# GpSimd without tensor work from routing on, and mish through one sigmoid, in a fused attention, expert and feed-forward kernel

## The chip, the cores and the metric

The kernel runs on one core of a Trainium2 chip. The metric is device time in microseconds (us), the median of several executions. The five engines of the core have queues of their own, each worked through strictly in the order in which the program wrote it, and they meet through semaphores: TensorE (PE in the profile; its weight loads are PEld), VectorE (DVE), ScalarE (ACT), GpSimd (POOL) and SyncE (SP), which here only starts DMA transfers.

## The reference

Three stages follow each other, each on the output of the one before. What is computed, shortened:

```
# 1. attention, 8 heads, 768 tokens, head_dim 64; only pairs in the same hash bucket count
scores = where(q_bucket == k_bucket, (q @ k.T) / 8, -1e9)
attn   = exp(scores - max);  attn /= sum + 1e-9
x      = attn @ v                                  # -> 768 x 512
# 2. mixture of 8 experts, top 1, at most 192 tokens an expert
logits = x @ w_gate;  expert = argmax(logits);  gate = softmax(logits)[expert]
y      = gate * (relu(x_e @ w1[e]) @ w2[e])        # w1: 8 x 512 x 1024, w2: 8 x 1024 x 512
# 3. a feed-forward network with mish
h      = y @ w_in                                  # 512 x 2048
sp     = where(h > 20, h, log1p(exp(min(h, 20))))
out    = (h * tanh(sp)) @ w_out                    # 2048 x 512
```

`w1` and `w2` come as float32, `w_in` and `w_out` as float64.

## The kernel before, in words

**Products in three terms.** Every float32 matrix that TensorE multiplies is split in two: a high part rounded to the type that TensorE takes (fp32r), and a low part, the rest. A product is three products: high by high, high by low, low by high. So each weight is loaded, its high part is cast (`wh`) and its low part subtracted (`wl`).

**Weights.** A chunk holds 1024 numbers per partition. Its raw numbers land in one of seven buffers (`raw`), which comes free when `wl` has been made. The high and low parts go into rings of six chunks. A float32 chunk of the experts (the key `w1` or `w2`) takes one cast (L573 on ScalarE or L575 on VectorE) and one subtraction (L580, on VectorE or GpSimd). A chunk of the second network (`wi`, `wo`) is float64 and comes in two halves; VectorE first rebuilds the float32 bits with three integer operations for each half (L552 and L554 in `w_bits`, L559 in `w_sign`), then follow cast and subtraction on 128x512. There are 64 chunks of the experts and 16 (32 halves) of the network. The first 13 chunks are loaded during attention, and the first six split there too.

**Routing.** From the logits VectorE works out each token's expert and its row there (L893 to L989, one-hot selection matrices `dg` at L947 among them); GpSimd then scatters the rows of x to memory (L953), from which SyncE loads them expert by expert (L1033).

**Experts.** In a step of the loop TensorE runs layer 1 of expert e+1 (L1064, 24 products with 512 columns) and layer 2 of expert e (L1106, 24 products with 512 columns), with transposes between (L1047): of the loaded rows, of the hidden units, and of the result. ScalarE and VectorE split each transposed block (`xh`/`xl`, `mhh`/`mhl`, `x2h`/`x2l`). Branches (L1198, L1152, L1166) skip rows beyond the first 128 of an expert where there are none. ScalarE also does relu (L1087) and the gate (L1123).

**Second network.** Sixteen steps f of 128 hidden units. Layer 1 of a step has two halves of 384 tokens, each of 12 products into one of two PSUM banks (`pg`, L1232); each half is then copied to the tile `hs_g` (L1242 on ScalarE or L1244 on VectorE), which frees the bank. mish then works on 128x768 numbers, and its result is split into `gh` (L1273) and `gl` (L1276). Layer 2 of a step has six token tiles of three products (`po`, L1282), which add up over all steps. Six tiles of `hs_g` exist, given back at `gl`: layer 1 of step f+6 cannot be copied out before `gl` of step f. There are four buffers `e_g`, four `n_g`, and the seven of `gh`/`gl`.

mish before, from h/2, with e = exp(min(h, 20)) and n = e(e + 2): mish = h n/(n + 2), where 1/(n/2 + 1) is exp(-ln(n/2 + 1)). For each step: `em` (VectorE), `e1` exp (ScalarE), `nn` (VectorE), `ln` (ScalarE), `e2` exp (ScalarE), `nm` (GpSimd, L1265, a product), `hm` (VectorE, L1268). A change between exp and ln makes ScalarE load another table first (ACT_TABLE_LOAD).

**What sets the order.** A planner (`Planner.run`) writes the queues. Each task has a duration for each engine that may do it, tasks that it waits for, and buffers that it takes and gives. Of all tasks that could begin, the one that could begin first by these durations is written next; a table of tuned numbers (`WHEN`, `FIRST`, `THEN`) only decides between those that could begin within 0.03 us of each other. `convert` makes the tasks of the weights, `expert_tasks` routing and experts, `network_tasks` the second network. In the second network the tasks of mish are tied in pairs of steps by `pair`.

## Time and profile before

| what | value |
|---|---|
| median of 3 runs (lowest to highest) | 484.14 us (482.75 to 484.5) |
| span of the profiled execution, first to last instruction | 481.0 us |
| median less that span | 3.1 us |
| PE, PEld busy | 426.2 us, 377.6 us |
| DVE, ACT, POOL busy | 407.6 us, 281.7 us, 196.7 us |
| mean granted TensorE clock | 0.951 |
| DMA over the span | 65.13 MB, mean 135 GB/s |

The profiled execution's own time is its span; no other time is listed for it, and the 3.1 us up to the median lie outside of what the trace shows. By TensorE's own instructions the span falls into attention (to about 154 us), routing (to 167), the experts (to 311), the second network (311 to 476) and the output (to 481). In a row of the timeline stand start, duration, engine, line, operation, what is written and read, and in square brackets how long the engine had been idle and what ended that. A row of a window gives its length, then for each engine the busy time and the number of instructions, then the granted TensorE clock, the DMA share and GB/s. In a row of groups stand busy time and mean duration in ns, then idle time before.

### The profile page before, as it was taken

The page shows a single profiled execution, that of the slowest core. Times are in us where ns is not written, and L with a number is a line of the kernel's source. Part 1 is how long each engine was busy: PE and PEld are TensorE (multiplying, and loading weights), DVE is VectorE, ACT ScalarE, POOL GpSimd, SP SyncE. Part 2 cuts the span into 40 slices and gives each one's busy share as a digit, 9 for nine tenths or more (in the row PEclk, how much of TensorE's full clock was granted, in tenths as well). Part 3 has the DMA queues.
Part 4 walks back from the last instruction along what each step waited for, and adds up shares of the span by engine and source line. Part 5 has one row for each costly group of instructions (what it writes and reads, how often), then busy time and mean ns, then how long its engine had stood idle before and what let it go on. Part 6 is the DMA issues. An engine that isn't in the chain of part 4 may idle for free. (4 is left out here: it accounts for less than half of the span.)

```text
span 481.0 us, 7356 instructions
## 1 busy us (share of the span) xinstructions
PE 426.2 (89%) x2628; PEld 377.6 (78%) x2628; DVE 407.6 (85%) x560; ACT 281.7 (59%) x483; POOL 196.7 (41%) x173
## 2 busy tenths in 40 slices
PE   7999999999999789899889895789697698599995
PEld 6999999999998767667667674788595697598784
DVE  6699999889886874949499999999999989999940
ACT  3598897787776234434445642428573674674552
POOL 5866575321001580406154524451518117107335
PEclk9799999999999899899999998889989599799998
DMA  6352532423000367958378878454213204200003
GB/s 183 116 181 85 163 117 83 133 68 106 5 1 1 133 172 232 347 191 275 124 269 277 303 272 310 142 191 167 104 49 131 90 0 174 89 0 1 0 0 131
DMA packets 30136, 65.13 MB, mean 135 GB/s; under 512 B 4752, under 2 KB 7824, under 8 KB 30096
## 3 DMA queue, kind: packets, MB, share of 16 engines
q1 hardware_dynamic: 28944, 61.44, 38.9%
q0 software_dynamic: 1152, 3.16, 1.7%
q8 instruction: 24, 0.39, 0.3%
q14 instruction: 16, 0.13, 0.1%
HBM read 58.26 MB, written 6.33 MB: 134 GB/s over the span
## 5 line engine op out<-in xcount | busy, mean ns | idle before, releaser
L580 POOL TENSOR_TENSOR wl<-raw,wh 128x1024 fp32r<-128x1024 f32 (+1 forms) x43 | 92.6, 2161 | 162.7 <-ACT wh L573 137.8
L573 ACT CAST wh<-raw 128x1024 fp32r<-128x1024 f32 (+1 forms) x70 | 59.8, 874 | 38.1 <-DVE raw L559 30.6
L580 DVE TENSOR_TENSOR wl<-raw,wh 128x1024 fp32r<-128x1024 f32 (+1 forms) x53 | 78.3, 1503 | 1.4 <-ACT wh L573 1.2
L1232 PE MATMUL pg<-x2h,wh 128*128 128x384 f32 x128 | 46.8, 365 | 11.9 <-ACT hs_g L1242 7.1
L700 DVE TENSOR_REDUCE nm<-ps 128x1 f32<-128x768 f32 x48 | 45.5, 950 | 6.8 <-PE ps L694 6.5
L732 DVE TENSOR_TENSOR atl<-pt,ath 128x512 fp32r<-128x512 f32 x72 | 46.7, 683 | 3.6 <-ACT ath L727 3.5
L1232 PE MATMUL pg<-x2l,wh 128*128 128x384 f32 x128 | 45.8, 358 | 2.5 <-DVE x2l L1145 2.5
L708 ACT ACTIVATE a<-ps,nm 128x768 f32<-128x768 f32 x48 | 44.1, 918 | 4.4 <-DVE nm L700 4.4
L1232 PE MATMUL pg<-x2h,wl 128*128 128x384 f32 x128 | 45.2, 353 | 0.0
L727 ACT CAST ath<-pt 128x512 fp32r<-128x512 f32 x72 | 39.0, 595 | 6.9 <-PE pt L722 6.5
L1282 PE MATMUL po<-wh,gh 128*128 128x512 f32 x96 | 38.1, 397 | 5.1 <-ACT gh L1273 5.1
L1265 POOL TENSOR_TENSOR n_g<-n_g,e_g 128x768 f32<-128x768 f32 x16 | 33.6, 2119 | 19.1 <-ACT e_g L1262 19.0
L1282 PE MATMUL po<-wh,gl 128*128 128x512 f32 x96 | 37.9, 395 | 2.4 <-DVE gl L1276 2.4
L722 PE MATMUL pt<-identf,a 128*128 128x128 f32 x288 | 38.5, 275 | 0.2 <-ACT a L708 0.2
L1282 PE MATMUL po<-wl,gh 128*128 128x512 f32 x96 | 37.9, 395 | 0.0
L744 PE MATMUL pa<-ath,vn 128*128 128x256 f32 x144 | 37.4, 295 | 0.5 <-ACT ot L632 0.5
L1232 PEld LDWEIGHTS pg<-x2h,wh 128*128 128x128 f32 x128 | 26.0, 203 | 14.1 <-ACT hs_g L1242 8.4
L554 DVE SCALAR_TENSOR_TENSOR raw<-raw,full 128x512 int32<-128x512 int32 x32 | 35.1, 1098 | 2.0
L744 PE MATMUL pa<-atl,vn 128*128 128x256 f32 x144 | 35.5, 282 | 0.0
L575 DVE CAST wh<-raw 128x1024 fp32r<-128x1024 f32 x26 | 27.2, 1060 | 7.4 <-PE ph L1064 4.7
L722 PEld LDWEIGHTS pt<-identf,a 128*128 128x128 f32 x288 | 32.1, 141 | 1.4 <-ACT a L708 0.5
L1106 PE MATMUL py<-wh,mhh 128*128 128x512 f32 (+1 forms) x72 | 28.1, 391 | 0.9 <-ACTq L1166 0.6
(199 smaller groups left out, 1086.1 us busy)
## 6 DMA issues: line engine op xcount, KB each, us to landing
raw<-in_moe_w_dram SPq DMA_DIRECT2D x64, 512.0 KB, 4.7
raw<-in_moe_w_in_dram SPq DMA_DIRECT2D x16, 512.0 KB, 4.2
raw<-in_moe_w_out_dram SPq DMA_DIRECT2D x16, 512.0 KB, 3.9
slots<-zt SPq DMA_DIRECT2D x12, 258.0 KB, 4.6
xs<-slots SPq DMA_DIRECT2D x8, 258.0 KB, 7.2
rq<-in_q_dram SPq DMA_DIRECT2D x8, 192.0 KB, 2.6
rk<-in_k_dram SPq DMA_DIRECT2D x8, 192.0 KB, 4.3
rv<-in_v_dram SPq DMA_DIRECT2D x8, 192.0 KB, 2.5
```

What stands on the lines that cost most here:

```text
L554: nc.vector.scalar_tensor_tensor(out=low, in0=low, scalar=29, in1=fl, op0=ALU.logical_shift_right, op1=ALU.bitwise_or)
L573: nc.scalar.copy(out=wt[c][0][:, sl], in_=val)
L580: eng_of[eng].tensor_tensor(out=wt[c][1][:, sl], in0=val, in1=f32(wt[c][0][:, sl]), op=ALU.subtract)
L700: r = nc.vector.tensor_reduce(out=nm, in_=d["ps", i][:, :, :HW], axis=AX.XY, op=ALU.max, negate=True)
L708: nc.scalar.activation(out=a, in_=d.pop(("ps", i))[:, :, :HW], func=AF.Exp, bias=d["nm", i], accum_out=d["rs"][:, i:i + 1])
L722: nc.tensor.transpose(pt[:, j, :], a[:, kt * P:(kt + 1) * P], identf)
L727: nc.scalar.copy(out=d["ath", g][:, sl, :], in_=d["pt", g, u])
L732: nc.vector.tensor_tensor(out=d["atl", g][:, sl, :], in0=d["pt", g, u], in1=f32(d["ath", g][:, sl, :]), op=ALU.subtract)
L744: nc.tensor.matmul(d["pa", g], lhsT=d["vn"][:, kt, :], rhs=mv, start=(kt == 0 and n == 0), stop=(kt == NT - 1 and n == 1))
L1232: mm = nc.tensor.matmul(pg[:, :HW], lhsT=st[:, kt, fs], rhs=mv[:, kt, j * HW:(j + 1) * HW], start=(kt == 0 and i == 0), stop=(kt == KD - 1 ...
L1265: eng_of[eng].tensor_tensor(out=n["n", f], in0=n["n", f], in1=n["e", f], op=ALU.mult)
L1282: nc.tensor.matmul(po[t], lhsT=st, rhs=mv[:, f % 2, :], start=(f == 0 and i == 0), stop=(f == NF - 1 and i == 2))
```

## The change

From routing on, GpSimd does no arithmetic on tensors. All low parts of weights (`wl`) are VectorE's, two chunks of the routing stage among them, and all high parts (`wh`) ScalarE's. mish is h sigmoid(h + ln(1 + e/2)), with the same e: n/(n + 2) is the sigmoid of ln(n/2), and n/2 = e(1 + e/2), whose logarithm is h + ln(1 + e/2). For each step that leaves `em`, `e1`, `ln`, then one sum `u` (VectorE, L1258), a sigmoid `sg` on ScalarE (L1261) and the product `hm` (VectorE, L1264); `nn` and GpSimd's `nm` are gone, and the buffers `n_g` with them. The sigmoid is in another table than exp and ln. The copy out of PSUM no longer halves. The planner is given 1.38, 2.09 and 0.69 us for products where it had 1.3, 1.95 and 0.65, and slightly other times for the conversions; two orders are added among the tasks of layer 1 and `gh`. The tuned numbers stay, and none stands for `u` and `sg`.

```diff
@@ expert_tasks
-            add(("l1", e, j), {"PE": 1.3 / n}, have + done["w1", e, k] + [("l1", e, j - 1)] * (j > 0),
+            add(("l1", e, j), {"PE": 1.38 / n}, have + done["w1", e, k] + [("l1", e, j - 1)] * (j > 0),
@@ convert
-            add(("wl", c, i), {"Pool": 1.23, "DVE": 0.6}, [("wh", c, i)], (), ["raw"], at)
+            add(("wl", c, i), {"DVE": 0.62}, [("wh", c, i)], (), ["raw"], at)
     elif c >= WA:
-        add(("wh", c), {"ACT": 0.95} if c < hold else {"ACT": 0.95, "DVE": 0.6},
+        add(("wh", c), {"ACT": 0.9},
...
-        add(("wl", c), {"Pool": 2.3} if early else {"DVE": 1.13} if c < hold else {"Pool": 2.3, "DVE": 1.13},
+        add(("wl", c), {"DVE": 1.14},
@@ network_tasks
-                add(("f1", f, j, i), {"PE": 1.95 / n}, [("yl", E - 1, i if n > 1 else 1)] + done["wi", f // 2] + [("f1", f, j, i - 1)] * (i > 0),
+                add(("f1", f, j, i), {"PE": 2.09 / n}, [("yl", E - 1, i if n > 1 else 1)] + done["wi", f // 2] + [("f1", f, j, i - 1)] * (i > 0),
                     ["g"] * (i == 0), ["a"] if f % 2 and j else (), b + 1.95 * (j + i),
-                    soft=[("yt", E - 1, 1)] * (f == 0))
+                    soft=[("yt", E - 1, 1)] if f == 0 else [("f1", f - 1, 1, 1 if f == 1 else 0)] if j == 0 else [("f1", f, 0, 0)])
...
-        add(("nn", f), {"DVE": 0.87}, [("e1", f)], ["nb"], (), b + 13)
-        pair = [("nn", x) for x in ((f - f % 2, f - f % 2 + 1) if f < NF - 2 else (f,))]
+        pair = [("e1", x) for x in ((f - f % 2, f - f % 2 + 1) if f < NF - 2 else (f,))]
         add(("ln", f), {"ACT": 0.74}, pair, (), (), p + 14, table="l")
-        add(("e2", f), {"ACT": 0.74}, [("ln", f)], (), (), p + 15, table="e")
-        add(("nm", f), {"Pool": 1.77}, [("e2", f)], (), ["eb"], b + 16)
-        add(("hm", f), {"DVE": 0.87}, [("nm", f)], (), ["nb"], b + 18)
-        add(("gh", f), {"ACT": 0.7}, [("hm", f)], ["gb"], (), b + 19)
+        add(("u", f), {"DVE": 0.87}, [("ln", f)], (), (), b + 16)
+        both = [("u", x) for x in ((f - f % 2, f - f % 2 + 1) if f < NF - 2 else (f,))]
+        add(("sg", f), {"ACT": 0.74}, both, (), (), p + 15, table="s")
+        add(("hm", f), {"DVE": 0.87}, [("sg", f)], (), ["eb"], b + 18)
+        add(("gh", f), {"ACT": 0.7}, [("hm", f)], ["gb"], (), b + 19, soft=[("gh", f - 1)] * (f > 0))
...
-            add(("s", f, t), {"PE": 0.65}, after, (), (["gb"] + ["a"] * (f % 2)) if t == NT - 1 else (), w)
+            add(("s", f, t), {"PE": 0.69}, after, (), (["gb"] + ["a"] * (f % 2)) if t == NT - 1 else (), w)
@@ mish
-        nc.vector.tensor_scalar(out=n["e", f], in0=n["hs", f], scalar1=2.0, scalar2=20.0, op0=ALU.mult, op1=ALU.min)
+        nc.vector.tensor_scalar(out=n["e", f], in0=n["hs", f], scalar1=20.0, scalar2=None, op0=ALU.min)
...
-        nc.scalar.activation(out=n["e", f], in_=n["n", f], func=AF.Ln, scale=0.5, bias=1.0)
-
-    def mish_inv(f, eng):
-        nc.scalar.activation(out=n["e", f], in_=n["e", f], func=AF.Exp, scale=-1.0)
+        nc.scalar.activation(out=n["e", f], in_=n["e", f], func=AF.Ln, scale=0.5, bias=1.0)
+
+    def mish_sum(f, eng):
+        nc.vector.tensor_tensor(out=n["e", f], in0=n["e", f], in1=n["hs", f], op=ALU.add)
 
     def mish_ratio(f, eng):
-        eng_of[eng].tensor_tensor(out=n["n", f], in0=n["n", f], in1=n["e", f], op=ALU.mult)
+        nc.scalar.activation(out=n["e", f], in_=n["e", f], func=AF.Sigmoid)
 
     def mish_out(f, eng):
-        nc.vector.tensor_tensor(out=n["hs", f], in0=n["hs", f], in1=n["n", f], op=ALU.mult)
+        nc.vector.tensor_tensor(out=n["hs", f], in0=n["hs", f], in1=n["e", f], op=ALU.mult)
```

The orders move at three places of which the prediction speaks. The first is VectorE's queue in one step of the experts, from one branch L1198 to the next. Before:

```order
L575 CAST wh<-raw 128x1024 x2
L580 TENSOR_TENSOR wl<-raw,wh 128x1024 x2
L1145 ISA
L1145 TENSOR_TENSOR x2l<-px,x2h 128x4x128
L575 CAST wh<-raw 128x1024
L1100 TENSOR_TENSOR mhl<-px,mhh 128x512 x2
L580 TENSOR_TENSOR wl<-raw,wh 128x1024
L1024 TENSOR_LOAD regs
L580 TENSOR_TENSOR wl<-raw,wh 128x1024
```

and now:

```order
L580 TENSOR_TENSOR wl<-raw,wh 128x1024 x2
L1145 ISA
L1145 TENSOR_TENSOR x2l<-px,x2h 128x4x128
L1100 TENSOR_TENSOR mhl<-px,mhh 128x512
L580 TENSOR_TENSOR wl<-raw,wh 128x1024
L1100 TENSOR_TENSOR mhl<-px,mhh 128x512
L580 TENSOR_TENSOR wl<-raw,wh 128x1024
L1024 TENSOR_LOAD regs
```

The casts L575 have left the queue, and a subtraction now stands between the two `mhl`. Over a whole step VectorE had about four casts and five subtractions, and now has eight subtractions; ScalarE has eight casts where it had about four.

The second place is ScalarE's queue at the end of the second network, the last two steps of mish. Before:

```order
L1259 ACT_TABLE_LOAD
L1259 ACTIVATE e_g<-n_g 128x768 x2
L1262 ACT_TABLE_LOAD
L1262 ACTIVATE e_g<-e_g 128x768 x2
L1273 CAST gh<-hs_g 128x768 x2
```

and now:

```order
L1252 ACT_TABLE_LOAD
L1252 ACTIVATE e_g<-e_g 128x768 x2
L1255 ACT_TABLE_LOAD
L1255 ACTIVATE e_g<-e_g 128x768 x2
L1261 ACT_TABLE_LOAD
L1261 ACTIVATE e_g<-e_g 128x768 x2
L1269 CAST gh<-hs_g 128x768 x2
```

Here the round of exp, ln and sigmoid takes three table loads where exp and ln took two. Over the second network there were 10 loads and are now 17.

The third place is VectorE's queue where the first steps of mish end. TensorE's queue there has changed with it: before, it held layer 1 of nine steps (0 to 8) ahead of the first product of layer 2; now it holds six steps (0 to 5), then layer 2 of six steps (36 tiles), then layer 1 of steps 6 to 14, one tile, step 15, and the 59 tiles that are left. VectorE now, from the first sums `u` to the first `gl`:

```order
L1258 TENSOR_TENSOR e_g<-e_g,hs_g 128x768 x2
L1244 COPY hs_g<-pg 128x384
L1258 TENSOR_TENSOR e_g<-e_g,hs_g 128x768 x2
L580 TENSOR_TENSOR wl<-raw,wh 128x512
L552 TENSOR_SCALAR full<-raw 128x512
L554 SCALAR_TENSOR_TENSOR raw<-raw,full 128x512
L1264 TENSOR_TENSOR hs_g<-hs_g,e_g 128x768 x2
L1249 TENSOR_SCALAR e_g<-hs_g 128x768 x2
L1264 TENSOR_TENSOR hs_g<-hs_g,e_g 128x768 x2
L559 SCALAR_TENSOR_TENSOR raw<-raw 128x512
L1272 TENSOR_TENSOR gl<-hs_g,gh 128x768 x4
```

Four steps of mish go through together, and the four `gl` come at its end; before, mish began with two steps, whose `gl` stood apart.

More of the change, by code (lines that the diff above doesn't have):

```diff
@@ L242, in expert_tasks @@
             gone = ["hb"] * ((k + 1) * FU % K2 == 0 and j // K2 == n - 1) + [place["w2", e, k]] * (last and j >= K2)
-            add(("l2", e, j), {"PE": 1.3 / n}, [("hl", e, k * FU // K2)] + done["w2", e, k] + [("l2", e, j - 1)] * (j > 0),
+            add(("l2", e, j), {"PE": 1.38 / n}, [("hl", e, k * FU // K2)] + done["w2", e, k] + [("l2", e, j - 1)] * (j > 0),
                 ["y"] if k == 0 else (), gone, b + TURN + 5.2 + 1.3 / n * j,
@@ L268, in convert @@
         for i in range(2):
-            add(("ca", c, i), {"DVE": 1.07}, [("dm", c)], when=at)
-            add(("cb", c, i), {"DVE": 0.6}, [("ca", c, i)], when=at)
+            add(("ca", c, i), {"DVE": 1.05}, [("dm", c)], when=at)
+            add(("cb", c, i), {"DVE": 0.62}, [("ca", c, i)], when=at)
             add(("wh", c, i), {"ACT": 0.52}, [("cb", c, i)] + ([("wh", c, 0)] if i else before), [place] * (i == 0), when=at)
-            add(("wl", c, i), {"Pool": 1.23, "DVE": 0.6}, [("wh", c, i)], (), ["raw"], at)
+            add(("wl", c, i), {"DVE": 0.62}, [("wh", c, i)], (), ["raw"], at)
     elif c >= WA:
-        add(("wh", c), {"ACT": 0.95} if c < hold else {"ACT": 0.95, "DVE": 0.6},
+        add(("wh", c), {"ACT": 0.9},
             [("dm" if c >= WA + RAW else "wd", c)] + before + [("lm",)] * (c < hold), [place], when=at)
         early = c < WA + 2
-        add(("wl", c), {"Pool": 2.3} if early else {"DVE": 1.13} if c < hold else {"Pool": 2.3, "DVE": 1.13},
+        add(("wl", c), {"DVE": 1.14},
             [("wh", c)] + [("ls",) if early else ("po",)] * (c < hold), (), ["raw"], at)
@@ L1012, in _body @@
     go(routing, fill=1e9)
-    planner.more(h=3, g=2, hg=HB, eb=EB, nb=EB, gb=LAG + 1)
+    planner.more(h=3, g=2, hg=HB, eb=EB, gb=LAG + 1)
     rctx.close()
@@ L1235, in first, with hidden @@
                     tc.declare_no_dep(mm.ins, late_y["l" if i == 1 else "h"].ins, reason="rows of the other half")
-    def halve(f, j, eng):
+    def hidden(f, j, eng):
         if j == 0:
@@ L1241, in halve @@
         if eng == "ACT":
-            nc.scalar.activation(out=dst, in_=src, func=AF.Copy, scale=0.5)
+            nc.scalar.copy(out=dst, in_=src)
         else:
-            nc.vector.tensor_scalar(out=dst, in0=src, scalar1=0.5, scalar2=None, op0=ALU.mult)
+            nc.vector.tensor_copy(out=dst, in_=src)
     def mish_min(f, eng):
         n["e", f] = gw.tile([P, 2, HW], F32, tag="e", name="e_g", bufs=EB)
-        nc.vector.tensor_scalar(out=n["e", f], in0=n["hs", f], scalar1=2.0, scalar2=20.0, op0=ALU.mult, op1=ALU.min)
+        nc.vector.tensor_scalar(out=n["e", f], in0=n["hs", f], scalar1=20.0, scalar2=None, op0=ALU.min)
     def mish_exp(f, eng):
         nc.scalar.activation(out=n["e", f], in_=n["e", f], func=AF.Exp)
-    def mish_n(f, eng):
-        n["n", f] = gw.tile([P, 2, HW], F32, tag="n", name="n_g", bufs=EB)
-        nc.vector.scalar_tensor_tensor(out=n["n", f], in0=n["e", f], scalar=2.0, in1=n["e", f], op0=ALU.add, op1=ALU.mult)
     def mish_ln(f, eng):
-        nc.scalar.activation(out=n["e", f], in_=n["n", f], func=AF.Ln, scale=0.5, bias=1.0)
-    def mish_inv(f, eng):
-        nc.scalar.activation(out=n["e", f], in_=n["e", f], func=AF.Exp, scale=-1.0)
+        nc.scalar.activation(out=n["e", f], in_=n["e", f], func=AF.Ln, scale=0.5, bias=1.0)
+    def mish_sum(f, eng):
+        nc.vector.tensor_tensor(out=n["e", f], in0=n["e", f], in1=n["hs", f], op=ALU.add)
     def mish_ratio(f, eng):
-        eng_of[eng].tensor_tensor(out=n["n", f], in0=n["n", f], in1=n["e", f], op=ALU.mult)
+        nc.scalar.activation(out=n["e", f], in_=n["e", f], func=AF.Sigmoid)
     def mish_out(f, eng):
-        nc.vector.tensor_tensor(out=n["hs", f], in0=n["hs", f], in1=n["n", f], op=ALU.mult)
+        nc.vector.tensor_tensor(out=n["hs", f], in0=n["hs", f], in1=n["e", f], op=ALU.mult)
     def g_hi(f, eng):
@@ L1293, in scatter_o @@
         sc_o.append(scatter(out, ids, lambda t: n["o", t])(t, eng))
-    do.update(f1=first, hs=halve, em=mish_min, e1=mish_exp, nn=mish_n, ln=mish_ln, e2=mish_inv, nm=mish_ratio, hm=mish_out,
+    do.update(f1=first, hs=hidden, em=mish_min, e1=mish_exp, ln=mish_ln, u=mish_sum, sg=mish_ratio, hm=mish_out,
               gh=g_hi, gl=g_lo, s=second, ob=out_copy, os=scatter_o)
```

## The prediction

> **What bounds the kernel now.** First windows by stage: length, busy us of PE, PEld, DVE, ACT, POOL, then clock, DMA share, GB/s.
>
> ```profile
> 155.00:167.00 12.00, 8.73 (x88) 8.33 (x85) 10.27 (x37) 3.61 (x6) 7.09 (x7) 0.86 0.32 111
> 167.00:237.00 70.00, 62.48 (x293) 46.20 (x292) 46.90 (x48) 29.08 (x44) 26.94 (x24) 0.98 0.70 228
> 237.00:283.00 46.00, 40.50 (x193) 30.99 (x192) 45.27 (x40) 24.26 (x34) 21.91 (x9) 1.00 0.78 266
> 283.00:311.00 28.00, 21.06 (x118) 18.05 (x116) 26.76 (x29) 11.65 (x19) 11.83 (x7) 0.88 0.72 247
> 311.00:476.00 165.00, 142.92 (x674) 127.06 (x672) 146.24 (x167) 95.29 (x136) 63.94 (x42) 0.93 0.23 80
> ```
>
> From 237 to 311 VectorE is busy 72.0 of 74 us, in the network 146.2 of 165. TensorE, whose products end the span, idles 5.5, 6.9 and 22.1 us in the last three windows. So I next looked in the timeline at what VectorE does with that time, beside GpSimd.
>
> ```profile
> 258.62 2.40 POOL L580 TENSOR_TENSOR wl<-raw,wh 128x1024 fp32r<-128x1024 f32 x1 [4.76 <-DVE wh L575]
> 259.61 2.49 DVE L580 TENSOR_TENSOR wl<-raw,wh 128x1024 fp32r<-128x1024 f32 x1
> 262.62 1.21 DVE L580 TENSOR_TENSOR wl<-raw,wh 128x1024 fp32r<-128x1024 f32 x1
> ...
> 356.50 0.42 DVE L552 TENSOR_SCALAR full<-raw 128x512 int32<-128x512 int32 x1
> 357.56 1.29 DVE L559 SCALAR_TENSOR_TENSOR raw<-raw 128x512 int32<-128x512 int32 x2
> ...
> 361.78 6.36 POOL L1265 TENSOR_TENSOR n_g<-n_g,e_g 128x768 f32<-128x768 f32 x3 [1.37 <-ACT e_g L1262]
> 362.09 2.08 DVE L552 TENSOR_SCALAR full<-raw 128x512 int32<-128x512 int32 x1
> ```
>
> The same subtraction takes VectorE 2.49 us while GpSimd works on one, and 1.21 us before GpSimd's next one begins; L552 takes 2.08 us in GpSimd's product and 0.42 us without. VectorE stands still for about as long as GpSimd's operation lasts: its busy time is partly waiting. Who waits for VectorE is in SyncE's waits (us, times, longest) and in TensorE's idle times:
>
> ```profile
> SPq L543 <- DVE wl L580: 43.7, 20, 4.2
> ```
>
> ```profile
> 198.63 1.08 PE L1047 MATMUL px<-identf,xs 128*128 128x128 f32 x4 [2.30 <-DMA xs<-slots]
> 299.60 1.94 PE L1047 MATMUL px<-identf,hsb 128*128 128x128 f32 x8 [4.13 <-DVEq L1198]
> 314.00 0.45 PE L1232 MATMUL pg<-x2l,wh 128*128 128x384 f32 x1 [2.52 <-DVE x2l L1145]
> 374.61 0.80 PE L1282 MATMUL po<-wh,gh 128*128 128x512 f32 x1 [5.14 <-ACT gh L1273]
> 414.03 0.69 PE L1232 MATMUL pg<-x2h,wh 128*128 128x384 f32 x1 [6.37 <-ACT hs_g L1242]
> ```
>
> Loads of weights wait 43.7 us for raw buffers that VectorE still needs, and TensorE's long waits are behind VectorE or behind ScalarE's work on what VectorE made late. (The loads of rows for 198.63 are behind those weights in SyncE's queue.)
>
> **The change part by part.** The sum is made against the span of 481.0 us; the median of the runs is 3.1 us above it.
>
> *A, routing.* GpSimd's two subtractions go, VectorE gets them.
>
> ```profile
> 154.84 4.84 POOL L580 TENSOR_TENSOR wl<-raw,wh 128x1024 fp32r<-128x1024 f32 x2
> 155.38 4.91 DVE L947 TENSOR_TENSOR dg<-cols,sel 128x256 f32<-128x256 f32 x3
> 159.88 0.41 DVE L947 TENSOR_TENSOR dg<-cols,sel 128x256 f32<-128x256 f32 x1
> 162.81 0.21 DVE L927 TENSOR_TENSOR sel<-pr,oh 128x48 f32<-128x48 f32 x1 [0.84 <-PE pr L910]
> 163.89 0.17 DVE L939 TENSOR_TENSOR slot_i<-s,dumpc 128x6 int32<-128x6 f32 x1
> ```
>
> The three `dg` took 4.91 us; three of 0.41, less 0.08 of overlap each, take 1.1, so what follows is 3.8 us earlier. The two subtractions stand before `sel` and `r`: 2.3 us, of which the 0.84 that `sel` waited is hidden. `slot_i`, and with it the scatter and all loads of rows, comes 3.8 - 2.3 + 0.84 = 2.4 us earlier: **-2.4** (bounds 0 and -3.8).
>
> *B, C, D, experts.* Rates of TensorE, and two results of the gate one step of two experts apart:
>
> ```profile
> 183.62 0.39 PE L1064 MATMUL ph<-wl,xh 128*128 128x512 f32 x1
> 188.63 0.40 PE L1064 MATMUL ph<-wh,xl 128*128 128x512 f32 x1
> 215.35 1.04 PE L1047 MATMUL px<-identf,hsb 128*128 128x128 f32 x8
> 249.05 0.69 ACT L1123 ACTIVATE ysb<-py,xs 128x512 f32<-128x512 f32 x1 [4.08 <-PEq L1198]
> 254.93 1.05 ACT L573 CAST wh<-raw 128x1024 fp32r<-128x1024 f32 x1
> 280.44 0.69 ACT L1123 ACTIVATE ysb<-py,xs 128x512 f32<-128x512 f32 x1 [4.03 <-PEq L1198]
> ```
>
> Between the first two lie 22 products: 0.228 us each. A step has 48, 10.9 us, and 16 transposes at 1.04/8, 2.1 us: 13.0 in all. It takes (280.44 - 249.05)/2 = 15.7. After the change VectorE has eight subtractions of 1.21 and four evacuations of 0.65, 12.3 us; ScalarE gets 13 casts of 1.05 in window 237 to 283, (24.26 + 13.7)/3 = 12.6 a step, off VectorE's queue but in its own; DMA, at 0.78 share for three steps of 15.3, needs 12.0. Four resources at 12 to 13 us will not run at 13.0; between 13.0 and 15.4 (the window's own 46/3) I take 14.0, nearer TensorE's rows since no engine then is over 93% busy: three steps, **-4.2** (bounds 0 and -7.2). Window 167 to 237 has the extra products of an overflowing expert and is TensorE's for 62 of 70 us; I take the wait of 2.30 at 198.63 in part, **-2.0** (0 and -7.5). Window 283 to 311 has GpSimd over VectorE for 11.8 us and TensorE idle for 6.9 at a clock of 0.88; the wait of 4.13 goes and a little with it: **-5.0** (0 and -6.9).
>
> *E, network.* Rates without GpSimd, and after a wait of TensorE:
>
> ```profile
> 318.11 0.34 PE L1232 MATMUL pg<-x2h,wh 128*128 128x384 f32 x1
> 325.74 0.34 PE L1232 MATMUL pg<-x2h,wl 128*128 128x384 f32 x1
> 349.65 0.52 PE L1232 MATMUL pg<-x2l,wh 128*128 128x384 f32 x1
> 349.97 0.52 PE L1232 MATMUL pg<-x2h,wl 128*128 128x384 f32 x1
> ...
> 379.26 0.55 DVE L1249 TENSOR_SCALAR e_g<-hs_g 128x768 f32<-128x768 f32 x1
> 379.73 0.95 DVE L1276 TENSOR_TENSOR gl<-hs_g,gh 128x768 fp32r<-128x768 f32 x1
> 380.60 0.94 DVE L1268 TENSOR_TENSOR hs_g<-hs_g,n_g 128x768 f32<-128x768 f32 x1
> 381.47 0.68 DVE L580 TENSOR_TENSOR wl<-raw,wh 128x512 fp32r<-128x512 f32 x1
> ...
> 352.87 0.49 ACT L1242 ACTIVATE hs_g<-pg 128x384 f32<-128x384 f32 x1 [0.85 <-PE pg L1232]
> 353.38 1.28 ACT L1259 ACT_TABLE_LOAD   x1
> 354.67 2.32 ACT L1259 ACTIVATE e_g<-n_g 128x768 f32<-128x768 f32 x3
> ```
>
> 44 products of layer 1 in 7.63 us are 0.174 each, a half 2.09; a tile of layer 2 is 3 x 0.228 = 0.69. Without any wait TensorE needs 32 x 2.09 + 96 x 0.69 = 133 us for what now takes the window's 165. After a wait, products begin 0.32 apart for some 3 us. On VectorE, by starts, `em` takes 0.47, `gl`, `hm` and the new sum 0.87, a subtraction 0.60; L552 with L554 1.06, L559 0.60. By these the work of 311 to 476 is about 115 us instead of 146: 27 halves of 1.66, 29 subtractions, 16 times 3.08 of mish, 9 copies of 0.47. On ScalarE a function takes 0.75 in a row of three and a table load 1.28. Seven loads more, 9.0 us, on an engine that idles 70 us there cost nothing in themselves, only where a copy out of PSUM stands behind them.
>
> I then walk the new queues from the first product, at 0. Layer 1 of steps 0 to 5 ends at 26 (25.1, and 0.9 of the wait of 2.52, whose cause was VectorE behind GpSimd). The 36 tiles that come next need `gl` of step 0. VectorE first has 11 subtractions, 8 halves of bits, 4 `em` and 2 copies, 22.7 us from 1.5 on, and 2.2 of waiting for step 3: the first sums end at 28.1, the table and two sigmoids at 29.9, and with the queue as it is written (two more sums, a subtraction, one L552 and L554, four `hm`, two `em`, one L559) `gl` of step 0 ends at 38. **TensorE waits 12 us there**, longer than any wait now, and starts again at half rate: 2. The tiles run 24.8, to 65; steps 4 and 5 are ready at 54, before they are wanted. Steps 6 to 14 take 37.6, with 3.3 of waits: VectorE has 23 us of conversions ahead of `em` of step 6, which comes at 77 and the copy of step 7 behind it, so step 8 waits 2.8; then copies and halves keep pace. One tile, step 15 and 59 tiles: 0.7 + 4.2 + 0.4 + 40.7, to 152. The last mish, with its three loads, ends near 134 and is wanted at 143, under the tiles. For the handing over between engines, 0.08 to 0.1 each by the overlap above and some 35 on this path, I add 3.5: 155.5 against 165, **-9.5**. Bounds: the 133 of TensorE (-32), and above: by the waits now, 22 us idle and 10 of slow clock, which stay if the wait of 12 doubles: 0.
>
> Sum: -2.4 - 2.0 - 4.2 - 5.0 - 9.5 = -23.1; 481.0 - 23.1 = 457.9 of span, and 3.1 for what lies around it: **461 us**.
>
> The Trainium skill speaks against the seventeen loads. "ScalarE: Activation LUTs", section What ACT_TABLE_LOAD costs, gives 1283 ns for the load and about 1380 ns more for a drain at each switch to another set. The load's row here agrees with 1.28; before it the copy L1242 ends at 353.36, 0.02 us ahead, and the next function starts 0.01 us behind it, so this trace has no drain. By the page, seventeen switches would hold ScalarE 23 us longer, nine of them (12 us) with TensorE waiting in steps 0 to 14: an estimate of 473 us.
>
> **The rivals.**
>
> *R1, the experts gain nothing.* Something else holds the step at 15.4: DMA at 0.78 share, ScalarE at 12.6. For it: ScalarE now casts all, and its queue waits for loads in order. Against: the loads themselves wait for VectorE. Without B, C and D: 472.
>
> *R2, the network gains nothing.* The wait of 12 us grows, or copies behind the table loads hold the two PSUM banks. For it: 414.03 is such a wait now, and the tuned numbers are of the old program. A table load that held ScalarE for twice its 1.28 would end here too: nine loads that stand before a wanted copy or before `gl` of step 0, 11.5 us more. Without E: 470 or 471; the page's estimate above is a case of it, and the rows leave it little of the chance.
>
> *R3, slower: ScalarE becomes the queue that all wait for.* Four casts more a step, in front of relu, gate and evacuations. If three of them (the ones that VectorE made in 0.6) end on TensorE's path, at 1.05, with no gain of C and D: 7 x 3.15 = +22, and the network as R2; 481.0 - 2.4 + 22 + 3.1 = 504; with E gained, 494. It decides once ScalarE is over nine tenths busy in the experts' steps; the forecast has 12.6 of 14.0, just at that.
>
> *R4, better.* Steps at 13.0 and half of the 12 us gone: 461 - 3 - 2 - 6 - 2 = 448.
>
> *R5, no difference*: R1, R2 and a lost A together: 484.
>
> **How the numbers follow.** Forecast 0.57 (own range 453 to 468), R1 0.14, R2 0.10, R3 0.08, R4 0.07, R5 0.04. A measurement of this kernel can tell about 0.5%, 2.4 us. Faster: 0.57 + 0.14 + 0.10 + 0.07 = 0.88; same 0.04; slower 0.08. The range of 449 to 478 holds the forecast, R1 and R2 with some spread, and about half of R4.
>
> **What would show it.** In the profile after: no arithmetic row on POOL from 155 on; L580 on VectorE near 1.2 us at 128x1024 and 0.68 at 128x512 everywhere (if not, GpSimd wasn't the cause); SyncE's wait for `wl` well under 43.7; results of the gate 14 us apart (15.5: R1); one wait of TensorE of about 12 us before the first product of layer 2, the longest; the network 155 us; 17 table loads of 1.28 without gaps around them. I am wrong if VectorE's share stays near 98% in the experts, if ScalarE's passes 90% with TensorE waiting for casts (R3), or if TensorE waits for copies out of PSUM for more than 10 us in steps 6 to 14 (R2).

## The result and the profile after

The changed kernel takes 463.77 us (median of five), the kernel before in the same set of runs 484.5: a ratio of 0.956, 95% interval 0.9521 to 0.96. A second set of runs gave 462.48 us (461.05 to 466.34), ratio 0.9541 (0.9482 to 0.96); the rows of "after" below are from its profile. Ratios leave out every run over 1.5% above the quickest of its kernel: one of the first set (690.61 us at a granted clock of 0.555, the one that was profiled; the other four took 462.87 to 464.09), one in experiment 8 (1408.18) and the two longest of four in experiment 2. The forecast was 461 us, its range 449 to 478.

The span went from 481.0 to 459.8 us. First the busy time by windows, as in the prediction (length, busy us of PE, PEld, DVE, ACT, POOL, then clock, DMA share, GB/s); the network's first product is now at 298.71, and the last copy of an output begins at 454.66:

```profile
155.00:167.00 12.00, 10.65 (x107) 9.50 (x104) 11.19 (x42) 5.86 (x11) 4.44 (x7) 1.00 0.46 151
167.00:237.00 70.00, 62.14 (x297) 46.52 (x296) 37.30 (x42) 38.99 (x56) 11.43 (x18) 0.98 0.70 231
237.00:283.00 46.00, 43.41 (x211) 34.86 (x210) 39.30 (x42) 38.14 (x52) 0.00 (x0) 1.00 0.93 315
283.00:298.71 15.71, 11.65 (x79) 9.93 (x78) 15.20 (x25) 7.97 (x14) 0.00 (x0) 1.00 0.53 187
298.71:454.66 155.95, 138.71 (x674) 124.58 (x672) 119.16 (x189) 100.13 (x134) 4.81 (x9) 0.93 0.27 91
```

GpSimd's arithmetic is gone; what is left on POOL are scatters, each with a memset of one column. VectorE does more operations than before and is busy less: 39.3 of 46 us where it was 45.3, and 119 us in the network where it was 146. ScalarE rose to 83% in the experts (38.1 of 46), TensorE to 94%, and DMA from a share of 0.78 to 0.93. The groups of the subtraction between row loads and the network show why; the first two rows are of before (VectorE, then GpSimd), the third is of after:

```profile
L580 DVE TENSOR_TENSOR wl<-raw,wh 128x1024 fp32r<-128x1024 f32 x40 | 65.0, 1655 | 0.1
L580 POOL TENSOR_TENSOR wl<-raw,wh 128x1024 fp32r<-128x1024 f32 (+1 forms) x20 | 49.6, 2485 | 81.7 <-ACT wh L573 58.1 <-DVE wh L575 23.6
```

```profile
L580 DVE TENSOR_TENSOR wl<-raw,wh 128x1024 fp32r<-128x1024 f32 (+1 forms) x55 | 64.0, 1211 | 17.9 <-ACT wh L573 17.9
```

VectorE does 55 subtractions (54 of them of 128x1024) in the time that 40 took beside GpSimd's 20: 1.21 us each on average instead of 1.66.

In the network TensorE has three waits of over 1 us (timeline, after):

```profile
330.43 0.79 PE L1278 MATMUL po<-wh,gh 128*128 128x512 f32 x1 [6.51 <-ACT gh L1269]
334.22 0.79 PE L1278 MATMUL po<-wh,gl 128*128 128x512 f32 x1 [2.57 <-DVE gl L1272]
369.73 0.69 PE L1232 MATMUL pg<-x2h,wl 128*128 128x384 f32 x1 [8.12 <-DVE wl L580]
```

The first two stand ahead of layer 2: 9.1 us, with one tile's first products between them. The third is in layer 1 of step 6, eight products in, and waits for a low part of weights.

By results of the gate (L1123 of each expert) the gain splits so, against the prediction's terms:

| stretch | before | after | gain | forecast |
|---|---|---|---|---|
| to the third result | 235.46 | 232.22 | 3.2 | A and B: 4.4 |
| third to sixth (three steps) | 44.98 | 41.49 | 3.5 | C: 4.2 |
| sixth to first network product | 30.63 | 25.00 | 5.6 | D: 5.0 |
| network, to the last output copy | 164.8 | 155.95 | 8.8 | E: 9.5 |
| all of it, by span | 481.0 | 459.8 | 21.2 | 23.1 |

These are rows of one execution each, and the first row of the table can't be told from nothing by them. In the seven kernels of this document whose queues are the same up to the third result (one of them with idle work on GpSimd), it comes between 232.22 (the execution shown here) and 236.05 us, where the kernel before had it at 235.46.

### The profile page after: what moved, and what is told of

Same layout as the page of the kernel before. It is cut to its first block, busy times and chain, and to the rows that moved or that the text cites. A ratio compares the mean times of both kernels' runs of the same rounds, so it can differ in the third digit from the quotient of the medians.

```text
span 688.8 us, 7268 instructions
## 1 busy us (share of the span) xinstructions
PE 659.8 (96%) x2630; PEld 487.8 (71%) x2630; DVE 360.7 (52%) x579; ACT 318.5 (46%) x508; POOL 83.0 (12%) x120
## 4 chain that ended last, share of the span: by engine, by line
issue 60%; POOL 2%; DMA 1%; POOLq 0%; SPq 0%
DMA idd<-tokid,pos_i 1%; POOL out_dram L953 1%; POOL idd L953 1%; DMA ids<-idd 0%; POOL apart L952 0%; POOLq L1321 0%; POOL slots L953 0%; POOLq L953 0%; SPq L968 0%
## 5 line engine op out<-in xcount | busy, mean ns | idle before, releaser
L580 DVE TENSOR_TENSOR wl<-raw,wh 128x1024 fp32r<-128x1024 f32 (+1 forms) x90 | 89.6, 1029 | 55.4 <-ACT wh L573 54.5
L573 ACT CAST wh<-raw 128x1024 fp32r<-128x1024 f32 (+1 forms) x96 | 85.1, 919 | 32.4 <-PE po L1278 19.4
L722 PE MATMUL pt<-identf,a 128*128 128x128 f32 x288 | 62.6, 391 | 0.0
L727 ACT CAST ath<-pt 128x512 fp32r<-128x512 f32 x72 | 42.2, 587 | 43.7 <-PE pt L722 42.4
L1278 PE MATMUL po<-wh,gh 128*128 128x512 f32 x96 | 55.8, 581 | 5.8 <-ACT gh L1269 5.8
L1232 PE MATMUL pg<-x2h,wh 128*128 128x384 f32 x128 | 61.3, 479 | 0.0
L1278 PE MATMUL po<-wh,gl 128*128 128x512 f32 x96 | 55.6, 579 | 2.9 <-DVE gl L1272 2.9
L744 PE MATMUL pa<-ath,vn 128*128 128x256 f32 x144 | 56.2, 403 | 0.5 <-ACT ot L632 0.5
L744 PE MATMUL pa<-atl,vn 128*128 128x256 f32 x144 | 53.2, 382 | 0.0
L708 ACT ACTIVATE a<-ps,nm 128x768 f32<-128x768 f32 x48 | 43.7, 910 | 4.5 <-DVE nm L700 4.4
L1106 PE MATMUL py<-wh,mhl 128*128 128x512 f32 (+1 forms) x72 | 38.3, 532 | 1.9 <-DVE mhl L1100 1.9
L1232 PEld LDWEIGHTS pg<-x2h,wl 128*128 128x128 f32 x128 | 28.3, 221 | 16.2 <-DVE wl L580 7.6
L1064 PE MATMUL ph<-wh,xh 128*128 128x512 f32 x64 | 37.9, 592 | 1.0 <-PEq L1166 0.4
L1106 PE MATMUL py<-wl,mhh 128*128 128x512 f32 (+1 forms) x72 | 38.6, 537 | 0.0
```

Source lines behind the costliest of these rows:

```text
L573: nc.scalar.copy(out=wt[c][0][:, sl], in_=val)
L580: eng_of[eng].tensor_tensor(out=wt[c][1][:, sl], in0=val, in1=f32(wt[c][0][:, sl]), op=ALU.subtract)
L708: nc.scalar.activation(out=a, in_=d.pop(("ps", i))[:, :, :HW], func=AF.Exp, bias=d["nm", i], accum_out=d["rs"][:, i:i + 1])
L722: nc.tensor.transpose(pt[:, j, :], a[:, kt * P:(kt + 1) * P], identf)
L727: nc.scalar.copy(out=d["ath", g][:, sl, :], in_=d["pt", g, u])
L744: nc.tensor.matmul(d["pa", g], lhsT=d["vn"][:, kt, :], rhs=mv, start=(kt == 0 and n == 0), stop=(kt == NT - 1 and n == 1))
```

## The experiments

Times are medians; ratios are to the kernel before, run beside them. The theory on trial was the prediction's: VectorE stands still while GpSimd works on a tensor, and the rest is dealing out the same work. The rivals were that only the share of the work matters, that the sigmoid's tables cost more than their loads, and, after the first runs, that the planner's new durations do part of it.

**1. The change again, and parts of it alone.** The first is the changed kernel itself:

> The changed kernel once more, for a profile at the full clock. Theory: time 461 to 466 us; in the trace one step of the experts about 14 us, SyncE's wait for the low parts well under 43.7 us, one wait of TensorE of about 12 us before the first product of layer 2, the network about 155 us. Rival (the gain is in other places than forecast): experts still 15.4 us a step and the network under 150, or the other way round.

Only the weights (`convert` without GpSimd, casts all ScalarE's; mish and durations of products as before):

```diff
-            add(("wl", c, i), {"Pool": 1.23, "DVE": 0.6}, ...
+            add(("wl", c, i), {"DVE": 0.6}, ...
-        add(("wh", c), {"ACT": 0.95} if c < hold else {"ACT": 0.95, "DVE": 0.6}, ...
+        add(("wh", c), {"ACT": 0.95}, ...
-        add(("wl", c), {"Pool": 2.3} if early else {"DVE": 1.13} if c < hold else {"Pool": 2.3, "DVE": 1.13}, ...
+        add(("wl", c), {"DVE": 1.13}, ...
```

> The kernel before with one part of the change: high parts of weights all ScalarE's, low parts all VectorE's; mish as before, with GpSimd's product. Theory (GpSimd's subtractions hold VectorE): routing and experts gain what the whole change gains there, 13.6 us, and the network a few us, since 25.7 us of GpSimd's subtractions leave it while 33.6 us of products stay: 466 to 471. Rival 1 (the experts are held by DMA or ScalarE): only routing gains, 480 to 483. Rival 2 (casts on ScalarE cost): 486 or more.

The same, and mish's product `nm` on VectorE, in the old form of mish:

```diff
-        add(("nm", f), {"Pool": 1.77}, [("e2", f)], (), ["eb"], b + 16)
+        add(("nm", f), {"DVE": 0.87}, [("e2", f)], (), ["eb"], b + 16)
```

> The kernel before with the weights as in the change, and mish by its old formula with GpSimd's product moved to VectorE. No tensor work on GpSimd from routing on, but two table loads a group and one more VectorE operation a step. Theory (the gain is that GpSimd no longer holds VectorE, whatever the formula): within 5 us of the whole change, 460 to 469. Rival (the new formula, with less VectorE work, makes the network's gain): the network near its old 165, in all 470 to 475.

The change with the weights dealt out as before (the three lines of the first diff turned round):

> The changed kernel with the weights' conversions dealt out as before (low parts on GpSimd or VectorE, high parts on ScalarE or VectorE), mish new. Theory: experts as before, since GpSimd still holds VectorE there; the network gains part, as 33.6 us of GpSimd's products are gone and its subtractions stay: 475 to 481. Rival (all is in the new mish): 464 to 470.

| kernel | us | ratio (95%) | first network product | network |
|---|---|---|---|---|
| after, again | 462.48 | 0.9541 (0.9482 to 0.96) | 298.7 | 156.0 |
| weights only | 468.37 | 0.9617 (0.9579 to 0.9656) | 305.7 | 160.4 |
| no GpSimd, old mish | 492.58 | 1.0133 (1.0096 to 1.017) | 306.5 | 179.7 |
| mish and durations, old dealing | 486.64 | 1.0027 (0.9996 to 1.0059) | 321.2 | 158.4 |

The kernel before took 485.9 us beside these. (The last two columns are from one profile each; that of "weights only" fell on its longest run, 473.06 us.) The weights alone bring three quarters of the gain (17.5 of 23.4 us by the medians), within the time expected, though its first network product is only 5.4 us earlier than before, not 13.6. The other part alone brings nothing in sum, where 475 to 481 or 464 to 470 us had been expected: its network is 6.4 us shorter, its experts are 10 us longer. And with GpSimd out of the old mish the kernel is 1.3% slower than before. That lies outside of both forecasts for it (460 to 469 and 470 to 475 us), so it is not enough, whatever the formula, that GpSimd no longer holds VectorE. Its network's waits of TensorE:

```profile
PE po L1282 <- ACT gh L1273: 29.0, 4, 13.9
```

29 us in four waits for `gh`: in this order the first tiles of layer 2 stand between steps of layer 1, ahead of what they need. How much of that is the order and how much VectorE's third pass of 0.87 a step was not separated. What two parts do together was not the sum of what each did, so something else had moved: the planner writes another order for each of them.

**2. The durations of before in the changed kernel.** No instruction is added or moved to another engine:

```diff
-            add(("l1", e, j), {"PE": 1.38 / n}, ...     # and l2
+            add(("l1", e, j), {"PE": 1.3 / n}, ...
...
-                add(("f1", f, j, i), {"PE": 2.09 / n}, ...
+                add(("f1", f, j, i), {"PE": 1.95 / n}, ...
...
-            add(("s", f, t), {"PE": 0.69}, ...
+            add(("s", f, t), {"PE": 0.65}, ...
```

(The five times of `convert` likewise.)

> The changed kernel, but the planner keeps the seven durations it had before (1.3, 1.95 and 0.65 us for products, 1.07/0.6, 0.95, 1.13, 0.6 for conversions). No instruction is added or removed; only the queues are written in another order, in the network layer 1 of steps 7 to 15 and layer 2 of the first steps alternate. Theory A (the durations are part of the gain, since the kernel with only the weights moved lost about 5 us in the first expert and 3 in the fourth against the changed kernel with the same engines for the same work): 468 to 482 us, with the first product of the network at 303 or later, and single waits for gh of more than 10 us among the first tiles of layer 2. Theory B (only the engines' work counts): 460 to 466 us.

It took 454.29 us by the median of four; the ratio, 0.9227 (0.9146 to 0.9307), is of the two shortest. Both theories were wrong, and mine in its sign. The four times lie far apart, 447.76, 451.93, 456.66 and 457.85 us, and the profile is of the third, so its rows count only where the runs in 7 agree with them. The first network product came at 305.79, 7 us later than in the change, as expected. But the network took 143.9 us instead of 156.0. TensorE's waits there:

```profile
PE po L1278 <- DVE gl L1272: 3.2, 1, 3.2
PE po L1278 <- ACT gh L1269: 2.5, 1, 2.5
PE pg L1232 <- DVE wl L580: 1.0, 1, 1.0
```

6.7 us instead of 17.2. With the old durations the planner writes layer 1 of steps 0 to 6, one tile, steps 7 to 10, and then tiles and steps in turn. One step more of layer 1 covers `gl` of step 0, and the weights of step 6, which the change has ready 71 us after the first product of the network, are ready by 33.

**3. Idle work on GpSimd in the network.** The order of all other engines is kept:

```diff
+        r_ = nc.scalar.activation(out=n["e", f], in_=n["e", f], func=AF.Ln, scale=0.5, bias=1.0)
...     # at step 0: three tiles z, two of them set to 0
+        g_ = nc.gpsimd.tensor_tensor(out=n["z"][2], in0=n["z"][0], in1=n["z"][1], op=ALU.mult)
+        tc.add_manual_dep(g_.ins, r_.ins.name, SYNC, reason="a product of no use, behind this logarithm")
```

> The changed kernel, every engine's order kept, and 16 products of no use of 128x768 on GpSimd, one behind each logarithm of mish, whose result nobody reads. Theory A (VectorE stands still while GpSimd works on a tensor): 16 x 1.8 to 2.1 us, some 32 us, are added to VectorE's 115 us of work in the network, rows of VectorE beside them take 1 to 2 us longer, and about a third to a half ends on the path, since VectorE's late copies and gl are what TensorE waits for: 470 to 480 us. Theory B (VectorE's idle time takes it, and GpSimd was in the way only by its own slowness): 461 to 466 us.

475.2 us, ratio 0.9741 (0.9692 to 0.979), where the change has 0.9541: 10 to 13 us lost to work that nobody waits for, as theory A had it. The groups of the network, the idle product and the sum `u`, and behind them the same sum in the change:

```profile
L1260 POOL TENSOR_TENSOR z_g<-z_g,z_g 128x768 f32<-128x768 f32 x16 | 38.2, 2390 | 117.0 <-ACT e_g L1255 116.2
L1264 DVE TENSOR_TENSOR e_g<-e_g,hs_g 128x768 f32<-128x768 f32 x16 | 30.5, 1950 | 5.2 <-ACT e_g L1255 5.2
L1270 DVE TENSOR_TENSOR hs_g<-hs_g,e_g 128x768 f32<-128x768 f32 x16 | 18.8, 1211 | 0.0
```

```profile
L1258 DVE TENSOR_TENSOR e_g<-e_g,hs_g 128x768 f32<-128x768 f32 x16 | 14.5, 954 | 5.3 <-ACT e_g L1255 5.3
```

The sums that stand beside the idle products take 1.95 us instead of 0.95. This shows by itself that GpSimd's work holds VectorE up: VectorE waits for no data, no buffer and no order of GpSimd's here. It is not held for all of GpSimd's time: VectorE's rows of the network are 25 us longer in all, beside 38.2 us of products.

**4. Idle work on GpSimd in the experts.** There is little memory free, so each group is six pieces of 128x176 on one small tile:

```diff
+        r_ = nc.scalar.copy(out=wt[c][0][:, sl], in_=val)
+        if not jobs[c][2] and c >= WA + 10 and c % 8 in (1, 4, 6):
+            for k in range(6):
+                g_ = nc.gpsimd.tensor_tensor(out=late["z"], in0=late["z"], in1=late["z"], op=ALU.subtract)
+                if k == 0:
+                    tc.add_manual_dep(g_.ins, r_.ins.name, SYNC, reason="work of no use, behind this cast")
...     # and the tile z, set to 0
```

> The changed kernel, every engine's order kept, and work of no use on GpSimd in the experts: behind 18 casts, three of every eight chunks, six subtractions of 128x176 each, whose result nobody reads. Theory A (VectorE stands still while GpSimd works): 18 groups of 2.4 to 3 us, 43 to 54 us, fall on VectorE, which has about 40 us free between 167 and 311; its rows beside them take 1 to 2 us longer, results of the gate come 15 us apart or more instead of 14.4, the first product of the network at 305 to 318, 468 to 482 us. Theory B (VectorE is not held up, or has the time): 461 to 466 us.

474.49 us, ratio 0.9737 (0.9696 to 0.9777); two results of the gate lie 15.05 us apart (246.03 and 276.13, two steps), the network begins at 305.77. Theory A's times held, but not its size (VectorE's rows were to take 1 to 2 us longer). The idle pieces, and the subtractions beside them:

```profile
L575 POOL TENSOR_TENSOR z_of<-z_of 128x176 f32<-128x176 f32 x105 | 93.3, 888 | 33.7 <-ACT wh L572 25.7
L582 DVE TENSOR_TENSOR wl<-raw,wh 128x1024 fp32r<-128x1024 f32 x54 | 74.4, 1422 | 14.0 <-ACT wh L572 14.0
```

93 us of GpSimd's time in short pieces cost VectorE's subtractions 54 x 0.21 = 11 us. In long pieces (before) 50 us cost 40 x 0.44 = 18 us.

**5. Fewer table loads.**

```diff
-        nc.scalar.activation(out=n["e", f], in_=n["e", f], func=AF.Sigmoid)
+        nc.scalar.activation(out=n["e", f], in_=n["e", f], func=AF.Exp)
```

> The changed kernel with exp in the place of the sigmoid: the output is not mish any more, the sigmoid is left out. The queues keep their order, and the network's table loads fall from 17 to 12. Theory A (a load costs its 1.28 us on an engine that has room): five loads less are 6.4 us of ScalarE, of which at most the two ahead of the first gl and one or two ahead of a wanted copy are on the path: 459 to 463 us. Theory B (each switch of table drains ScalarE and costs 2.66 us, and most are waited for): 448 to 456 us.

465.52 us (463.48 to 467.86), ratio 0.9564 (0.9509 to 0.9619): five loads less bring nothing, and the time is above both forecasts (459 to 463 and 448 to 456). The loads of the changed kernel's network, and two of them with their neighbours:

```profile
L1255 ACT ACT_TABLE_LOAD x6 | 7.7, 1283 | 0.1
L1261 ACT ACT_TABLE_LOAD x6 | 7.7, 1283 | 0.1
L1252 ACT ACT_TABLE_LOAD x5 | 6.4, 1283 | 0.1
```

```profile
410.02 1.28 ACT L1252 ACT_TABLE_LOAD   x1
411.31 3.05 ACT L1252 ACTIVATE e_g<-e_g 128x768 f32<-128x768 f32 x4
414.38 1.28 ACT L1255 ACT_TABLE_LOAD   x1
415.67 3.05 ACT L1255 ACTIVATE e_g<-e_g 128x768 f32<-128x768 f32 x4
```

17 loads of 1.283 us, 0.1 us idle before six of them together. The Trainium skill ("ScalarE: Activation LUTs", section What ACT_TABLE_LOAD costs) adds about 1380 ns for a drain at each switch. No row here has room for one, and the time without five of the switches did not fall.

**6. More buffers.** `HB = 8`, `EB = 6` instead of 6 and 4:

> The changed kernel with eight tiles hs_g instead of six and six e_g instead of four. The planner then writes layer 1 of steps 0 to 5, 28 tiles of layer 2, layer 1 of steps 6 to 15, the rest, with 11 table loads instead of 17. Theory A (the 8.1 us that TensorE waits in step 6 come from the six tiles hs_g and from the rounds of four steps of mish that they force): the wait of about 9 us before layer 2 stays, the one of step 6 shrinks to under 4: 455 to 460 us. Theory B (VectorE's conversions of weights set both waits): the wait moves, and the time stays within 460 to 466 us.

460.29 us, ratio 0.9437 (0.937 to 0.9505). This lies at the border of the two theories' times. The wait in step 6 is gone, as theory A had it, but the wait before layer 2, which was to stay at about 9, grew from 9.1 to 14.8:

```profile
PE po L1278 <- ACT gh L1269: 14.3, 1, 14.3
PE po L1278 <- DVE gl L1272: 0.5, 1, 0.5
```

With six tiles `e_g` more steps of mish go through together, and the first `gl` comes at the end of a longer row.

**7. The durations, taken apart.** The change, with the old durations only for the network, the float64 conversions and the last expert, so that the experts keep the order of the change:

```diff
-            add(("l1", e, j), {"PE": 1.38 / n}, ...     # and l2
+            add(("l1", e, j), {"PE": (1.38 if e < 7 else 1.3) / n}, ...
...
-                add(("f1", f, j, i), {"PE": 2.09 / n}, ...
+                add(("f1", f, j, i), {"PE": 1.95 / n}, ...
...
-            add(("s", f, t), {"PE": 0.69}, ...
+            add(("s", f, t), {"PE": 0.65}, ...
```

> The changed kernel, where only the network's two products, the float64 conversions and the products of the last expert have the durations of before. TensorE's, ScalarE's and SyncE's queues in the experts stay those of the change (but for some rows of the last expert), those of the network are nearly those of the kernel with all old durations: layer 1 of steps 0 to 6, one tile of layer 2, steps 7 to 10, then tiles and steps in turn. Theory A (the old durations lose 7 us in the experts and gain 12 in the network, and these are two separate things): first network product at 298 to 301, network 143 to 147, 446 to 452 us. Theory B (the network was quick there only since loads and conversions had 7 us more of a lead when it began): network 150 or more, 454 to 462 us.

454.16 us (452.37 to 456.6), ratio 0.9302 (0.9252 to 0.9352): the time lies in theory B's range. But the network took 145.4 us, as theory A had it: its order, not a lead, made it short. The first network product came at 303.17, later than theory A's 298 to 301. From the second result of the gate on it took 88.4 us, where the change took 87.7 and all durations old 91.6; the rest of the difference from the change is that the second result came at 214.77 instead of 210.97. That is no effect of the edit: in the seven kernels here whose queues are the same up to there the second result comes between 210.45 and 214.77, with waits of TensorE for the loads of rows of 1.5 us in the earliest and 7.4 in the latest. So the old durations bring the network 11 to 12 us, and what they cost the experts is not settled. The three kernels with that queue of the experts (2, and two of 1) have the first network product at 305.7 to 306.5, the four with the queue of the change up to there at 298.7 to 302.1, which is 4 to 8 us in the traces, a part of it in waits for rows. The times don't show it: the kernel with all old durations has the same median as this one (454.29), and two of its four runs were shorter than any here.

The same with eight tiles `hs_g` (and the float64 conversions as in the change):

> As the kernel with mixed durations, but the float64 conversions with the durations of the change and eight tiles hs_g instead of six: layer 1 of steps 0 to 8 stands ahead of the first tile of layer 2, and the network has 14 table loads instead of 17. Theory A (what TensorE waits for is the first gl, about 37 us after the first product of the network, and two more steps of layer 1 cover it): no wait over 3 us in the network, 138 to 142 us for it, 442 to 448 us in all. Theory B (VectorE's conversions are late whatever the order): the wait shows again behind wl or a copy out of PSUM, 449 to 457 us.

451.95 us (450.23 to 453.98), ratio 0.9255 (0.9209 to 0.9301), the lowest median that was run, 3% under the change by the two ratios (0.9541). All old durations (2), at a ratio of 0.9227, can't be told from it. Its network:

```profile
303.86:445.95 142.09, 136.76 (x674) 122.93 (x672) 116.00 (x182) 98.24 (x138) 4.57 (x9) 0.98 0.29 99
```

```profile
PE pg L1232 <- ACT wh L573: 4.0, 1, 4.0
PE pg L1232 <- DVE wl L580: 1.2, 2, 1.0
```

No wait is left ahead of layer 2; two steps more of layer 1 cover the first `gl`. What is left is 4.0 us behind a late conversion, and the time lies in theory B's range, so each theory had half of it. TensorE is busy 96% of this stretch, at a clock of 0.98.

**8. The new durations alone, on the kernel before.**

```diff
-            add(("l1", e, j), {"PE": 1.3 / n}, ...     # and l2, f1, s, ca, cb
+            add(("l1", e, j), {"PE": 1.38 / n}, ...
```

> The kernel before, with only the planner's durations of products and of the bits of float64 numbers as in the change (1.38, 2.09, 0.69, 1.05, 0.62 us); no work moves to another engine, GpSimd keeps its part of the weights and of mish. Theory A (the durations pay only where VectorE has room): 482 to 490 us. Theory B (in the experts they are a gain of their own, as they are on the changed split of the work): first network product 4 us or more earlier than 311, 472 to 481 us.

500.17 us (500.0 to 501.06), ratio 1.0257 (1.0216 to 1.0297): slower, beyond both theories. The first network product comes at 320.4, where the kernel with mish and durations but the old dealing (in 1) has it at 321.2 and the kernel before at 311.1. Up to the network the queues of these two kernels are the same, row by row, so the loss of 10 us in the experts is that of the durations, while GpSimd still has its part of the weights.

With this run the parts can be told apart. It differs from "mish and durations, old dealing" only by the new mish (with its two added orders): 500.17 against 486.64 us, so the new mish alone gains 13.5. "Weights only" and the kernel of 2 differ by the same, on the new dealing: 468.37 against 454.29, a gain of 14.1. Taken in this order, the change is by medians 17.5 us of weights and 14.1 of mish, less 8.2 that the new durations cost; the last two rest on the kernel of 2, whose times spread by 10 us.

## Why the prediction was right, and where it was not

**The sum held, in part by luck.** 21.2 us of span where 23.1 were forecast. No part is off by more than 1.2 us, but errors inside the largest one, E, cancel, and a part that was given no term costs 8 us (both below). The 3.1 us that the forecast added around the span are not all there: every run of the changed kernel's second set is 1.8 to 1.9 us longer than its span. The profiled execution of the kernel before took by that an estimated 482.8 us, about its quickest, and the forecast span alone would have given 459.7.

**What bounds the kernel: shown, with a limit.** VectorE's busy time was partly standstill; runs 3 and 4 bring it back without any other change. L580 takes 1.21 to 1.23 us in 128x1024 throughout, and 0.69 in 128x512. But "stands still for about as long as GpSimd's operation lasts" is too much: in run 3 it is 25 of 38.2 us, and some operations are not held at all. This row of before stands between the prediction's own rows (GpSimd's subtraction runs from 258.62 to 261.02):

```profile
258.41 1.27 DVE L1100 TENSOR_TENSOR mhl<-px,mhh 128x512 fp32r<-128x512 f32 x2
```

The two `mhl`, which read one operand from PSUM, take their usual 0.68 us each, and the subtraction behind them 2.49. In the experts before, 11 of the 16 `mhl` ran beside GpSimd's subtractions, and none took over 0.69. Why they go free was not tested.

**A (forecast 2.4): right where it was placed, and partly lost behind it.** These are VectorE's `dg` and `slot_i`, and the loads of rows, after:

```profile
155.47 1.10 DVE L947 TENSOR_TENSOR dg<-cols,sel 128x256 f32<-128x256 f32 x3
161.52 0.17 DVE L939 TENSOR_TENSOR slot_i<-s,dumpc 128x6 int32<-128x6 f32 x1
172.69 3.56 SPq L1033 DMA_DIRECT2D xs<-slots  x6
177.27 1.09 PE L1047 MATMUL px<-identf,xs 128*128 128x128 f32 x4 [2.59 <-DMA xs<-slots]
197.11 0.63 PE L1047 MATMUL px<-identf,xs 128*128 128x128 f32 x4 [1.78 <-DMA xs<-slots]
```

`slot_i` is 2.37 us earlier (163.89), the three `dg` take 1.10 as worked out, the loads start 1.7 us earlier (174.39). TensorE meets them sooner, and its wait for them grows from 1.26 to 2.59.

**B (2.0): under the mark.** The wait of 2.30 at 198.63, which it was to take away in part, is 1.78 now; A and B together gave 3.2 instead of 4.4 in this execution, and between 3.2 and -0.6 in the seven kernels with these queues: the gain of 4.4 is not shown.

**C (4.2): nearly, with one row of its reasoning wrong.** The step is 14.43 us:

```profile
244.84 0.69 ACT L1123 ACTIVATE ysb<-py,xs 128x512 f32<-128x512 f32 x1 [1.44 <-PEq L1198]
273.71 0.69 ACT L1123 ACTIVATE ysb<-py,xs 128x512 f32<-128x512 f32 x1 [2.50 <-PEq L1198]
```

```profile
244.84:273.71 28.87, 26.43 (x128) 21.03 (x128) 23.83 (x25) 22.45 (x30) 0.00 (x0) 1.00 0.96 332
249.05:280.44 31.39, 27.01 (x128) 20.80 (x128) 30.90 (x27) 16.13 (x22) 14.79 (x6) 1.00 0.85 294
```

(The second of these windows is the same two steps before.) The prediction gave DMA 12.0 us a step, from a share of 0.78. Two whole steps before have 0.85 x 15.7 = 13.3 us, and now 0.96 x 14.43 = 13.9: DMA (96% of these steps), not TensorE (92%), VectorE (83%) or ScalarE (78%), is nearest to the bound. That would also explain a sign that I had named and that did not come, though no run tests it. SyncE's waits for raw buffers did not fall "well under 43.7" (between 167 and 311, before and after):

```profile
SPq L543 <- DVE wl L580: 46.1, 21, 4.2
```

```profile
SPq L543 <- DVE wl L580: 41.6, 37, 2.9
```

They are more and shorter: with the DMA engines busy 96% of these steps, loads still wait for buffers.

**D (5.0): right**, 5.6.

**E (9.5): the sum right by luck, its two waits mis-sized.** The walk had 12 us before layer 2 and 3.3 in steps 6 to 14; the trace has 9.1 and 8.1. The first is the same mechanism, 3 us shorter. `gl` of step 0 lets TensorE go on 35.5 us after the first product, not 38, and the tiles end at 61.3, not 65. The step that failed is "VectorE has 23 us of conversions ahead of `em` of step 6": the conversions were counted, but only what stood behind them on VectorE. Step 6's own products need one of these conversions, and TensorE stands at it before any copy could:

```profile
368.38 0.69 DVE L554 SCALAR_TENSOR_TENSOR raw<-raw,full 128x512 int32<-128x512 int32 x1
368.99 0.69 DVE L580 TENSOR_TENSOR wl<-raw,wh 128x512 fp32r<-128x512 f32 x1
```

TensorE's product at 369.73 starts when the second row ends, and for 5.3 us runs at half the clock (length, busy times, then clock 0.50, DMA share, GB/s):

```profile
369.73:374.99 5.26, 5.26 (x17) 5.26 (x17) 3.81 (x7) 0.48 (x1) 0.00 (x0) 0.50 0.29 103
```

The last product of layer 2 starts 155.5 us after the first of the network, the forecast's figure for the end. Four errors cancel: the tiles end 3.7 us sooner than in the walk, the wait in step 6 is 4.8 longer than its 3.3, the slow clock behind it costs 2.5 that the walk did not have (17 products 0.32 apart instead of 0.174), and its 3.5 for handing over do not show.

**Table loads: right.** Run 5 shows that five of the seventeen are not on the path, and the estimate of 473 us did not come.

**What the prediction left out: the planner's durations.** It gave no term to the seven numbers. Run 8 prices five of them at +13 us on the old dealing of the work. On the new one they cost 8 us by the medians (runs 2 and 7): the network loses 11 to 12, since another order is written, and the experts gain some of it back. The walk of the new queues held that cost without naming it: it found the wait of 12 us, and did not ask whether the order that makes it came with the work or with the numbers. R1, R2 and R3 did not come. R2 is nearest in kind: the network gained nearly what was forecast (8.8), but the order that came with the numbers kept it from 11 to 12 us more. The forecast was met all the same because the walk went through the queues that those numbers had already written.

## What to carry to other kernels

A busy engine beside GpSimd's tensor work may be standing still: compare the duration of one and the same operation with and without it before moving work, and test it with GpSimd work that nobody reads. Where a planner writes the queues, its numbers are a part of the change of their own: run them alone, and look for waits that only the order makes (one engine held at the first result of a long chain, while later independent work stands behind it). When a change is of several parts, time the parts, and each pair of them if they meet in a planner: here two parts gained 17.5 and 14 us, and a third, seven numbers, cost 8.
